# Block transposes on VectorE for Q, gate and up, and W_down's products directly behind the last PV

## The chip, the cores and the metric

The kernel runs on one core of a Trainium2 chip. The metric is device time in microseconds (us) of one execution. Five engines matter here: PE (TensorE: matrix products, with PEld for its weight loads), DVE (VectorE), ACT (ScalarE), POOL (GpSimd) and SP (SyncE, which only issues the transfers here). Sixteen DMA engines move data from HBM to SBUF. Engines run their own instruction streams in order and meet only at semaphores. A line such as L344 is line 344 of the kernel's file.

## The reference

One decode step of a transformer block with attention and a gated FFN in parallel; 4 sequences, one new token each. bf16 in and out.

```python
xn = layernorm(x)                                  # x: [4, 1, 512]
q  = xn @ wq                                       # 512 x 4096: 32 heads of 128
k, v = the last 4096 of 16384 cached rows, 8 kv heads (4 query heads share one)
o  = softmax(q k^T / sqrt(128)) v
g  = silu(xn @ w_gate)                             # 512 x 1792
u  = xn @ w_up                                     # 512 x 1792
out = x + o @ wo + (g * u) @ w_down                # wo: 4096 x 512, w_down: 1792 x 512
```

The cached rows that are read are 64 MiB; the five weight matrices are 13.25 MiB.

## The kernel before

**Transfers.** SP issues all large transfers on one queue, in this order: W_Q, K of steps 0 and 1, W_gate, W_up, then V and K in turn for the 16 steps (`ND`), W_down, the last V in two halves, and W_O in four pieces (`WO_CUTS` = 0, 16, 26, 30, 32: of the 32 row blocks of W_O the pieces hold 16, 10, 4 and 2). A step takes one kv head of two sequences, 2 MiB of K and 2 MiB of V. K and V have two buffers each. SP waits for `s_tr` (the transposes of K two steps back) before it issues a K, and for `s_pv` (the products with V of the step before) before it issues a V. The last V and W_O stand behind the wait for `s_pv` = 16.

**Start.** Layernorm on four partitions, four small transposes to `XnT`, then Q: 32 products of 512 columns (L360 from L374; L360 is the line of the helper `mm`, so most products have it), in four column groups of the PE array, so that partition 32j+b of a PSUM bank holds sequence b's heads of group j. Since the later products need Q with the head's 128 elements on the partitions, the two banks are copied to `QB` as bf16 (ACT L266 and DVE L287 side by side), turned by eight transposes on PE (L378), and spread into `QZ` by four small copies on DVE (L294).

**Steps.** The loop on PE transposes K (L390), copied to `KT` by DVE (L302), takes scores (L360, tile `ps_s`), shifts them by the maxima, ACT takes the exponential (L269), and PE multiplies by V (tile `ps_o`). `norm` on DVE (L318 to L322) divides by the denominators and writes one head group into `OT`.

**End.** Behind the loop, PE runs the rest of the last steps in this written order:

1. products with V, first-half sums and shift of steps still open;
2. gate (16 products of 512 columns) and up (16 more), again in four column groups: partition 32j+b holds sequence b's features of group j. Of a row of W_gate the columns are taken as `(m u)`: four neighbours (`u`), then a step of 14 elements (`m`); group 3 repeats two of the 14 feature blocks so that all groups have 512 columns;
3. x into the accumulator `ps_acc`, the last step's denominators and 64 products with V;
4. wait `s_gu`; four transposes of `gu` (L468); wait `s_nrm`; four transposes of `OT` (L472); wait `s_ob`; four small products that spread `OB` (L360, tile `ps_kt<-oB,rep`);
5. wait `s_guT`; 28 products with W_down; wait `s_op`; 64 products with W_O, each piece behind its own semaphore `d_wo`. Both write `ps_acc`, two column groups at a time.

ACT takes exp(-gate) from PSUM (L271, 128 x 512). DVE makes silu(gate)*up from it in four operations on 128 x 512: add one (L337), reciprocal (L339), multiply by gate (L341), multiply by up with the write in another order (L344). Only partitions 32j to 32j+3 of each 32 hold data. Then, in this order, the last `norm`, the copy `OB` (L349), the copy `guT` (L351), the copy `OP` (L353), and the copy of the result to `y` (L355), which SP and ACT write out.

Of the kernel before, what the change touches and what calls it, by code (L numbers as in the profile page):

```python
# [3 lines left out]
BF16 = mybir.dt.bfloat16  # L4
FP32 = mybir.dt.float32
ALU = mybir.AluOpType
ACT = mybir.ActivationFunctionType
# [3 lines left out]
def bass_parallel_sum__sliding_block_cached__swiglu_ffn__decode_kernel(  # L11
# [12 lines left out]
    B, _, D = A_x.shape  # L24
    _, HKV, Sk, Dh = A_k_cache.shape
    HQ = A_wq.shape[1] // Dh
# [3 lines left out]
    NC = D // 128  # L30
    NF = F // 128
    REP = HQ // HKV
# [3 lines left out]
    C = 2 * REP  # L36
# [23 lines left out]
    KT = sb("kT", [128, 2 * HKN], BF16)  # L60
    P = sb("p", [128, 2 * PS], BF16)
    QZ = sb("qz", [128, ND, WIDE], BF16)
    ident = sb("ident", [128, 128], BF16)
# [15 lines left out]
    st_std = sb("st_std", [B, 1], FP32)  # L79
    st_rstd = sb("st_rstd", [B, 1], FP32)  # L80
    XnT = sb("xnT", [128, NC, 32], BF16)
    QB = sb("qB", [128, 2, 512], BF16)
    den = sb("den", [128, C], FP32)
    OT = sb("oT", [128, B, REP + HQ], BF16)
    OB = sb("oB", [32, B, Dh], BF16)
    OP = sb("oP", [128, NO, B], BF16)
    ex = WQ[:, 0:1024].bitcast(FP32)
    gu = sb("gu", [128, 4, 128], BF16)
    guT = sb("guT", [128, 4, 128], BF16)
    I4 = sb("i4", [B, B], FP32)  # L90
    I4w = sb("i4w", [B, 64], BF16)
    y = sb("y_sb", [128, 256], BF16)
# [9 lines left out]
    O_wide = ps_O[:, 0:WIDE]  # L102
    den_ps = ps_O[:, 128:256]
    xT_ps = ps_acc[:, 0:NC * B]
    q_ps = kt_ps[2]
    mt_ps = ps_acc[0:C, 0:128]
    gate_ps = ps_kt[0][:]
    up_ps = ps_kt[1][:]
    gu_ps = kt_ps[2][:, B:2 * B, :]
    tr_ps = kt_ps[2][0:32, 0:B, :]  # L110
    op_ps = ps_kt[3][:, 0:B * 32]

    def sem(name):
        return nc.alloc_semaphore(name=name)
    d_x = sem("d_x")
    d_wq = sem("d_wq")
    d_wg = sem("d_wg")
    d_wu = sem("d_wu")
    d_wd = sem("d_wd")
# [13 lines left out]
    s_xT = sem("s_xT")  # L133
    s_xnT = sem("s_xnT")
    s_q = sem("s_q")
    s_qb = sem("s_qb")
    s_qt = sem("s_qt")
    s_gu = sem("s_gu")
    s_gt = sem("s_gt")
    s_qz = sem("s_qz")  # L140
    s_tr = sem("s_tr")
# [9 lines left out]
    s_gate = sem("s_gate")  # L151
    s_ex = sem("s_ex")
    s_up = sem("s_up")
    s_guT = sem("s_guT")
# [20 lines left out]
    with nc.Block() as block:  # L175
# [78 lines left out]
        @block.scalar  # L254
        def _(eng):
            eng.dma_start(X[:], x_ap).then_inc(d_x, 16)
            eng.wait_ge(s_xc, 1)
            eng.activation(xc[:], X[:], ACT.Identity, bias=st_neg[:, 0:1], scale=float(D))
            eng.drain()
            eng.activation(xsq[:], xc[:], ACT.Square, accum_out=st_sum[:, 0:1]).then_inc(s_ss, 1)  # L260
            eng.wait_ge(s_var, 1)
            eng.activation(st_std[:], st_var[:], ACT.Sqrt).then_inc(s_std, 1)
            eng.wait_ge(s_rs, 1)
            eng.activation(xn[:], xc[:], ACT.Identity, scale=st_rstd[:, 0:1]).then_inc(s_xn, 1)  # L264
            eng.wait_ge(s_q, 1)
            eng.activation(QB[:, 0, :], ps_kt[0][:], ACT.Identity).then_inc(s_qb, 1)  # L266
            for d in range(-1, ND):
                eng.wait_ge(s_sh, d + 2)
                eng.activation(P[:, d % 2 * PS:d % 2 * PS + SN], ps_S[d % 2][:], ACT.Exp, scale=SCALE).then_inc(s_p, 1)  # L269
            eng.wait_ge(s_gate, 1)  # L270
            eng.activation(ex, gate_ps, ACT.Exp, scale=-1.0).then_inc(s_ex, 1)  # L271
            eng.wait_ge(s_y, 1)
            eng.dma_start(out_ap[1], y[64:64 + B, :]).then_inc(d_out, 16)

        @block.vector
        def _(eng):
# [6 lines left out]
            eng.wait_ge(s_xT, 1)  # L283
            eng.wait_ge(s_const, 1)
            eng.tensor_copy(XnT[:, :, 0:B], xT_ps.rearrange("p (c b) -> p c b", b=B)).then_inc(s_xnT, 1)
            eng.wait_ge(s_q, 1)
            eng.tensor_copy(QB[:, 1, :], ps_kt[1][:]).then_inc(s_qb, 1)  # L287
            eng.wait_ge(s_qt, 1)

            qv = q_ps.rearrange("p (n h) (j x) -> p j n x h", n=2, x=32)  # L290
            qz = QZ[:].rearrange("p (j n i) c -> p j n i c", n=2, i=2)
            for n in range(2):
                for i in range(2):
                    last = eng.tensor_copy(qz[:, :, n, i, 0:C].rearrange("p j (m h) -> p j m h", m=2),  # L294
                                           qv[:, :, n, 2 * i:2 * i + 2, :])
            last.then_inc(s_qz, 1)
            eng.engine_nop().then_inc(s_ev, NG)

# [17 lines left out]
            def norm(n, b, r):  # L316
                eng.wait_ge(s_pv, n)
                eng.tensor_reduce(den[:], den_ps.rearrange("p (t c) -> p c t", c=C), AX.X, ALU.add)  # L318
                eng.drain()
                eng.reciprocal(den[:], den[:])  # L320
                eng.drain()
                eng.tensor_tensor(OT[:, 2 * b:2 * b + 2, ds(r * REP, REP)],  # L322
                                  O_ps.rearrange("p (j h) -> p j h", j=2),
                                  den[:].rearrange("p (j h) -> p j h", j=2), ALU.mult).then_inc(s_nrm, 1)

            with eng.Fori(0, ND // 2) as r:
                for b in range(2):
# [5 lines left out]
            row_max(1, ND + 1)  # L333
            shift(ND + 1)
            norm(ND + 1, 0, ND // 2)
            eng.wait_ge(s_ex, 1)
            eng.tensor_scalar(ex, ex, 1.0, None, ALU.add)  # L337
            eng.drain()
            eng.reciprocal(ex, ex)  # L339
            eng.drain()  # L340
            eng.tensor_tensor(ex, gate_ps, ex, ALU.mult)  # L341
            eng.wait_ge(s_up, 1)
            eng.drain()
            eng.tensor_tensor(gu[:].rearrange("p u m -> p m u"), up_ps.rearrange("p (m u) -> p m u", u=4),  # L344
                              ex.rearrange("p (m u) -> p m u", u=4), ALU.mult).then_inc(s_gu, 1)
            norm(ND + 2, 1, ND // 2)

            eng.wait_ge(s_t4, 1)
            eng.tensor_copy(OB[:], tr_ps).then_inc(s_ob, 1)  # L349
            eng.wait_ge(s_gt, 1)  # L350
            eng.tensor_copy(guT[:], gu_ps).then_inc(s_guT, 1)  # L351
            eng.wait_ge(s_pm, 1)
            eng.tensor_copy(OP[:].rearrange("p c b -> p b c"), op_ps.rearrange("p (b c) -> p b c", b=B)).then_inc(s_op, 1)  # L353
            eng.wait_ge(s_acc, 1)
# [3 lines left out]
        def _(eng):  # L358
            def mm(o, l, r, start=False, stop=True):
                return eng.matmul(o, l, r, start=start, stop=stop, skip_group_check=True)  # L360
# [3 lines left out]
            for c in range(NC):  # L364
                last = eng.transpose(xT_ps[:, c * B:(c + 1) * B],  # L365
                                     xn[:].rearrange("b (p c) -> b c p", c=NC)[:, c, :], I4[:])
            last.then_inc(s_xT, 1)
            eng.wait_ge(s_xnT, 1)
            eng.wait_ge(d_wq, 16)
            for c in range(NC):  # L370
                for n in range(2):
                    for j in range(4):
                        a = (c * HQ + 8 * j + 4 * n) * Dh
                        last = mm(ps_kt[n][32 * j:32 * j + 32, :], XnT[:, c, :], WQ[:, a:a + 512], start=(c == 0))  # L374
            last.then_inc(s_q, 1)
            eng.wait_ge(s_qb, 2)
            for k in range(8):
                last = eng.transpose(q_ps[:, k, :], QB[:, k // 4, 128 * (k % 4):128 * (k % 4 + 1)], ident[:])  # L378
            last.then_inc(s_qt, 1)

            def mask(bank):
                return mm(ps_S[bank][:].rearrange("p (t c) -> p t c", c=C), mkr[:],
# [65 lines left out]
            pv(0, 1, ND + 1)  # L448
            shift(1, ND + 1)


            T0 = (0, 4, 8, NF - 4)
            for w, o, done, d in ((WG, ps_kt[0], s_gate, d_wg), (WU, ps_kt[1], s_up, d_wu)):
                eng.wait_ge(d, 16)
                for c in range(NC):
                    wv = w[:, c, :].rearrange("p (m t) -> p m t", t=NF)
                    for j in range(4):
                        last = mm(o[32 * j:32 * j + 32, :].rearrange("p (m u) -> p m u", u=4), XnT[:, c, :],
                                  wv[:, :, T0[j]:T0[j] + 4], start=(c == 0))
                last.then_inc(done, 1)  # L460
            for n in range(2):
                mm(ps_acc[64 * n:64 * n + 64, 0:256], I4w[:], X[:, 256 * n:256 * n + 256], start=True)
            pv(1, 0, (8 * ND + 16, ND + 1))
            eng.wait_ge(d_vz, 16)
            pv(1, 1, None)
            eng.wait_ge(s_gu, 1)
            for u in range(4):
                last = eng.transpose(gu_ps[:, u, :], gu[:, u, :], ident[:])  # L468
            last.then_inc(s_gt, 1)
            eng.wait_ge(s_nrm, ND + 2)  # L470
            for i in range(B):
                last = eng.transpose(  # L472
                    tr_ps[:, i, :],
                    OT[:, i, REP:], ident[:])
            last.then_inc(s_t4, 1)
            eng.wait_ge(s_ob, 1)
            for e in range(REP):
                last = mm(op_ps.rearrange("p (b c) -> p b c", b=B), rep[:, e, :], OB[:, :, 32 * e:32 * e + 32],
                          start=(e == 0))
            last.then_inc(s_pm, 1)  # L480
            eng.wait_ge(s_guT, 1)
            eng.wait_ge(d_wd, 16)
            for t in range(NF):
                j = min(t // 4, 3)
                u = t - T0[j]
                for n in range(2):
                    mm(ps_acc[64 * n:64 * n + B, 0:256], guT[:, u, 32 * j:32 * j + B],
                       WD[:, t, 256 * n:256 * n + 256])
            eng.wait_ge(s_op, 1)
            for c in range(NO):  # L490
                if c in WO_CUTS:
# [32 lines left out]
```

## Time and profile before

| | |
|---|---|
| median of 3 runs | 202.76 us (201.81 to 202.96) |
| the profiled execution's own time | 203.49 us |
| its span, first to last instruction | 201.8 us |
| PE, DVE, ACT, POOL busy | 83%, 59%, 9%, 5% of the span |
| HBM read | 81.01 MB, 402 GB/s over the span |
| mean granted TensorE clock | 0.958 |

In the page of the profile, the span is cut in 40 slices of 5.04 us. A digit is the busy share of a slice in tenths; PEclk is the clock granted to PE in tenths of full speed. A row of the chain of waits reads: start, duration, what ran (or what was waited for). A row of the timeline adds the number of instructions and, in brackets, how long the engine had been idle and what ended that. The views of the trace are from the profiled execution alone.

### The profile page before, as it was taken

The numbers are of one execution on the slowest core, as the hardware profiler recorded it, in microseconds if no ns is written. First come the engines' busy times: TensorE is split into PE (matmuls) and PEld (weight loads), VectorE is DVE, ScalarE is ACT, GpSimd is POOL, SyncE is SP. The second block draws the span as 40 slices with busy tenths as digits, with TensorE's granted clock in tenths as the row PEclk, the third lists the DMA queues.
The fourth block names the chain that finished last, engine by engine and source line by source line (L and its number), as shares of the span: only waits on it lengthen the run. The fifth ranks groups of instructions, "written<-read, shape, count | busy, mean of one in ns | idle before, by whom it ended". The sixth has DMA issues, their size and how long they took to land.

```text
span 201.8 us, 7765 instructions
## 1 busy us (share of the span) xinstructions
PE 167.1 (83%) x3470; PEld 143.2 (71%) x3470; DVE 119.3 (59%) x250; ACT 17.6 (9%) x27; POOL 10.3 (5%) x23
## 2 busy tenths in 40 slices
PE   0137998859999989889898989898989898986395
PEld 0113896758988978788788878887878787854263
DVE  1003757644777575757666767676767676738700
ACT  6303010101010101010100101010101010110000
POOL 8920000000000000000000000000000000000000
PEclk9999699988999999999999999999999999999559
DMA  7999999999999999999999999999999999999800
GB/s 248 448 393 429 436 424 426 437 422 429 406 426 439 435 422 439 432 422 435 432 432 426 439 435 422 439 432 422 435 432 432 426 439 435 413 435 421 373 12 1
DMA packets 5934, 81.10 MB, mean 402 GB/s; under 512 B 668, under 2 KB 680, under 8 KB 936
## 3 DMA queue, kind: packets, MB, share of 16 engines
q1 hardware_dynamic: 5912, 81.01, 94.4%
q8 instruction: 5, 0.08, 0.2%
q10 hardware_dynamic: 16, 0.01, 0.0%
q14 instruction: 1, 0.01, 0.0%
HBM read 81.01 MB, written 0.00 MB: 402 GB/s over the span
## 4 chain that ended last, share of the span: by engine, by line
DMA 51%; PE 40%; DVE 6%; issue 2%; ACT 0%; DVEq 0%
DMA kbuf<-in_A_k_cache_dram 44%; PE ps_kt L390 17%; PE ps_s L360 9%; DMA wq_sb<-in_A_wq_dram 6%; PE ps_o L360 6%; PE ps_acc L360 5%; PE ps_kt L360 3%; DVE wq_sb L339 2%; DVE kT L302 1%; DVE gu L344 1%; DVE rm L307 0%; DVE qB L287 0%; DVE wq_sb L341 0%; PE ps_kt L378 0%; ACT wq_sb L271 0%
## 5 line engine op out<-in xcount | busy, mean ns | idle before, releaser
L302 DVE COPY kT<-ps_kt 128x1024 bf16<-128x1024 bf16 x128 | 79.8, 683 | 27.3 <-PE ps_kt L390 27.2
L390 PE MATMUL ps_kt<-ident,kbuf 128*128 128x128 bf16 x1024 | 64.4, 222 | 10.6 <-DMA kbuf<-in_A_k_cache_dram 10.5
L390 PEld LDWEIGHTS ps_kt<-ident,kbuf 128*128 128x128 bf16 x1024 | 58.8, 99 | 15.6 <-issue 15.6
L360 PE MATMUL ps_o<-p,vbuf 128*128 128x64 bf16 x1120 | 39.4, 195 | 0.0
L360 PEld LDWEIGHTS ps_o<-p,vbuf 128*128 128x128 bf16 x1120 | 36.2, 99 | 1.2
L360 PEld LDWEIGHTS ps_s<-qz,kT 128*128 128x128 bf16 x1024 | 31.4, 98 | 7.6 <-issue 4.6
L360 PE MATMUL ps_s<-qz,kT 128*128 x1024 | 34.8, 192 | 2.0 <-issue 0.8
L269 ACT ACTIVATE p<-ps_s 128x512 bf16<-128x512 f32 x17 | 10.2, 597 | 152.0 <-PE ps_s L360 152.0
L307 DVE TENSOR_REDUCE rm<-ps_s 128x8 bf16<-128x512 f32 x17 | 11.8, 691 | 19.3 <-PE ps_s L360 19.3
L360 PE MATMUL ps_kt<-wq_sb,xnT 128*32 128x512 bf16 x32 | 3.4, 609 | 5.4 <-DMA wq_sb<-in_A_wq_dram 5.4
L360 PE MATMUL ps_o<-p,ones 128*128 128x128 bf16 (+1 forms) x69 | 6.9, 220 | 0.8 <-DVE qz L294 0.7
L360 PE MATMUL ps_s<-mkc,mkr 2*128 2x512 bf16 x17 | 6.7, 393 | 0.0
L365 PE MATMUL ps_acc<-i,xn 4*128 4x4 f32 x4 | 0.6, 255 | 7.2 <-ACT xn L264 7.2
L360 PE MATMUL ps_s<-dg,ones 8*128 8x512 bf16 x17 | 6.5, 385 | 0.0
L360 PEld LDWEIGHTS ps_kt<-wq_sb,xnT 128*32 128x32 bf16 x32 | 1.3, 140 | 6.9 <-issue 6.9
L318 DVE TENSOR_REDUCE den<-ps_o 128x8 f32<-128x128 f32 x18 | 5.1, 281 | 1.6 <-PE ps_o L360 1.6
L287 DVE CAST qB<-ps_kt 128x512 bf16<-128x512 f32 x1 | 0.7, 691 | 8.7 <-PE ps_kt L360 8.7
L365 PEld LDWEIGHTS ps_acc<-i,xn 4*128 4x128 f32 x4 | 0.6, 210 | 7.2 <-issue 7.2
L360 PEld LDWEIGHTS ps_o<-p,ones 128*128 128x128 bf16 x69 | 4.5, 98 | 1.3 <-issue 0.8
L211 POOL MEMSET vbuf<- 128x6144 f32 x1 | 5.2, 5222 | 0.0
L360 PE MATMUL ps_acc<-wo_sb,oP 128*4 128x256 bf16 x64 | 5.1, 334 | 0.0
L355 DVE CAST y_sb<-ps_acc 128x256 bf16<-128x256 f32 x1 | 0.4, 426 | 7.5 <-PE ps_acc L360 7.5
(69 smaller groups left out, 62.7 us busy)
## 6 DMA issues: line engine op xcount, KB each, us to landing
kbuf<-in_A_k_cache_dram SPq DMA_DIRECT2D x16, 2048.0 KB, 12.6
vbuf<-in_A_v_cache_dram SPq DMA_DIRECT2D x15, 2048.0 KB, 11.2
wq_sb<-in_A_wq_dram SPq DMA_DIRECT2D x1, 4096.0 KB, 12.3
vbuf<-in_A_v_cache_dram SPq DMA_DIRECT2D x2, 1024.0 KB, 9.2
wo_sb<-in_A_wo_dram SPq DMA_DIRECT2D x1, 2048.0 KB, 14.5
wg_sb<-in_B_w_gate_dram SPq DMA_DIRECT2D x1, 1792.0 KB, 25.8
wu_sb<-in_B_w_up_dram SPq DMA_DIRECT2D x1, 1792.0 KB, 29.4
wd_sb<-in_B_w_down_dram SPq DMA_DIRECT2D x1, 1792.0 KB, 15.0
```

Source lines behind the costliest of these rows:

```text
L211: eng.memset(VB[:, HKN:].bitcast(FP32), 0.0)
L269: eng.activation(P[:, d % 2 * PS:d % 2 * PS + SN], ps_S[d % 2][:], ACT.Exp, scale=SCALE).then_inc(s_p, 1)
L287: eng.tensor_copy(QB[:, 1, :], ps_kt[1][:]).then_inc(s_qb, 1)
L302: eng.tensor_copy(KT[:, u * HKN + 1024 * g:u * HKN + 1024 * (g + 1)], kt_ps[g].rearrange("p a b -> p (a b)")).then_inc(s_ev, 1)
L307: eng.tensor_reduce(RM[:], ps_S[bank][:].rearrange("p (t c) -> p c t", c=C), AX.X, ALU.max).then_inc(s_rm, 1)
L318: eng.tensor_reduce(den[:], den_ps.rearrange("p (t c) -> p c t", c=C), AX.X, ALU.add)
L339: eng.reciprocal(ex, ex)
L344: eng.tensor_tensor(gu[:].rearrange("p u m -> p m u"), up_ps.rearrange("p (m u) -> p m u", u=4), ex.rearrange("p (m u) -> p m u", u=4), AL ...
L355: eng.tensor_copy(y[:], ps_acc[:, 0:256]).then_inc(s_y, 1)
L360: return eng.matmul(o, l, r, start=start, stop=stop, skip_group_check=True)
L365: last = eng.transpose(xT_ps[:, c * B:(c + 1) * B], xn[:].rearrange("b (p c) -> b c p", c=NC)[:, c, :], I4[:])
L390: last = eng.transpose(kt_ps[g][:, k, :], KB[:, a:a + 128], ident[:])
```

## The change

Q, gate and up are turned by VectorE's 32x32 block transposes, straight out of PSUM as float32. A block transpose turns each block of 32 partitions by 32 columns in place: element (32j+b, 32t+m) goes to (32j+m, 32t+b).

- **Q.** The products are ordered so that the first bank is complete after 16 of the 32 (with `s_q` raised for each bank), and take their columns in blocks of 32 neighbours, so that after the block transposes (two, 128 x 512) each head's 128 elements lie on the 128 partitions. Two copies spread the result into `QZ`. The copies to `QB` on ACT and DVE, the eight PE transposes and two of the four copies into `QZ` go.
- **Gate and up.** 16 products each of 448 columns instead of 512 (nothing repeated). Columns are taken as `(t m)`: the inner index `m` runs over 32 columns with a step of 14 elements (28 bytes), each column by itself. DVE turns gate to `gT` and, once up is there, up to `uT` (128 x 448 each, into the storage of W_Q). The four batch columns of each of 14 feature blocks are then 56 columns on all 128 partitions. ACT's exponential now reads `gT` and waits for its transpose (`s_gt`) instead of the gate products; add, reciprocal and both multiplications are on 56 columns, and the last writes `guT` directly. The four PE transposes of `gu` and the copy to `guT` go.
- **Order at the end.** W_down's 28 products stand right behind the last products with V, ahead of the transposes of `OT`; before, they stood ahead of W_O's.

```diff
-    QB = sb("qB", [128, 2, 512], BF16)
...
-    ex = WQ[:, 0:1024].bitcast(FP32)
-    gu = sb("gu", [128, 4, 128], BF16)
-    guT = sb("guT", [128, 4, 128], BF16)
+    ex = sb("ex", [128, NF, B], FP32)
+    guT = sb("guT", [128, NF, B], BF16)
+    qT = KT[:, 0:2048].bitcast(FP32)
+    gT = WQ[:, 0:NF * 64].bitcast(FP32)
+    uT = WQ[:, NF * 64:NF * 128].bitcast(FP32)
...
-    gate_ps = ps_kt[0][:]
-    up_ps = ps_kt[1][:]
+    gate_ps = ps_kt[0][:, 0:NF * 32]
+    up_ps = ps_kt[1][:, 0:NF * 32]
...
 # ACT
-            eng.wait_ge(s_q, 1)
-            eng.activation(QB[:, 0, :], ps_kt[0][:], ACT.Identity).then_inc(s_qb, 1)
             for d in range(-1, ND):
...
-            eng.wait_ge(s_gate, 1)
-            eng.activation(ex, gate_ps, ACT.Exp, scale=-1.0).then_inc(s_ex, 1)
+            eng.wait_ge(s_gt, 1)
+            eng.activation(ex[:], gT.rearrange("p (t b) -> p t b", b=32)[:, :, 0:B], ACT.Exp, scale=-1.0).then_inc(s_ex, 1)
...
 # DVE, start
-            eng.wait_ge(s_q, 1)
-            eng.tensor_copy(QB[:, 1, :], ps_kt[1][:]).then_inc(s_qb, 1)
-            eng.wait_ge(s_qt, 1)
...
             for n in range(2):
-                for i in range(2):
-                    last = eng.tensor_copy(qz[:, :, n, i, 0:C].rearrange("p j (m h) -> p j m h", m=2),
-                                           qv[:, :, n, 2 * i:2 * i + 2, :])
+                eng.wait_ge(s_q, n + 1)
+                eng.transpose(qT[:, 512 * n:512 * n + 512], ps_kt[n][:])
+            eng.drain()
+            for i in range(2):
+                last = eng.tensor_copy(
+                    QZ[:].rearrange("p (k i) c -> p k i c", i=2)[:, :, i, 0:C].rearrange("p k (m h) -> p k m h", m=2),
+                    qT.rearrange("p (k h x) -> p k x h", h=REP, x=32)[:, :, 2 * i:2 * i + 2, :])
             last.then_inc(s_qz, 1)
...
 # DVE, end
             norm(ND + 1, 0, ND // 2)
+
+            eng.wait_ge(s_gate, 1)
+            eng.transpose(gT, gate_ps).then_inc(s_gt, 1)
+            eng.wait_ge(s_up, 1)
+            eng.transpose(uT, up_ps)
             eng.wait_ge(s_ex, 1)
-            eng.tensor_scalar(ex, ex, 1.0, None, ALU.add)
-            eng.drain()
-            eng.reciprocal(ex, ex)
-            eng.drain()
-            eng.tensor_tensor(ex, gate_ps, ex, ALU.mult)
-            eng.wait_ge(s_up, 1)
-            eng.drain()
-            eng.tensor_tensor(gu[:].rearrange("p u m -> p m u"), up_ps.rearrange("p (m u) -> p m u", u=4),
-                              ex.rearrange("p (m u) -> p m u", u=4), ALU.mult).then_inc(s_gu, 1)
+            eng.tensor_scalar(ex[:], ex[:], 1.0, None, ALU.add)
+            eng.drain()
+            eng.reciprocal(ex[:], ex[:])
+            eng.drain()
+            eng.tensor_tensor(ex[:], gT.rearrange("p (t b) -> p t b", b=32)[:, :, 0:B], ex[:], ALU.mult)
+            eng.drain()
+            eng.tensor_tensor(guT[:], uT.rearrange("p (t b) -> p t b", b=32)[:, :, 0:B], ex[:],
+                              ALU.mult).then_inc(s_guT, 1)
             norm(ND + 2, 1, ND // 2)
...
-            eng.wait_ge(s_gt, 1)
-            eng.tensor_copy(guT[:], gu_ps).then_inc(s_guT, 1)
...
 # PE, start
-            for c in range(NC):
-                for n in range(2):
+            for n in range(2):
+                for c in range(NC):
+                    wv = WQ[:, c * HQ * Dh:(c + 1) * HQ * Dh].rearrange("p (n h d) -> p n h d", n=2, d=Dh)
                     for j in range(4):
-                        a = (c * HQ + 8 * j + 4 * n) * Dh
-                        last = mm(ps_kt[n][32 * j:32 * j + 32, :], XnT[:, c, :], WQ[:, a:a + 512], start=(c == 0))
-            last.then_inc(s_q, 1)
-            eng.wait_ge(s_qb, 2)
-            for k in range(8):
-                last = eng.transpose(q_ps[:, k, :], QB[:, k // 4, 128 * (k % 4):128 * (k % 4 + 1)], ident[:])
-            last.then_inc(s_qt, 1)
+                        last = mm(ps_kt[n][32 * j:32 * j + 32, :].rearrange("p (h d) -> p h d", d=32), XnT[:, c, :],
+                                  wv[:, n, :, 32 * j:32 * j + 32], start=(c == 0))
+                last.then_inc(s_q, 1)
...
 # PE, end
-            T0 = (0, 4, 8, NF - 4)
-            for w, o, done, d in ((WG, ps_kt[0], s_gate, d_wg), (WU, ps_kt[1], s_up, d_wu)):
+            for w, o, done, d in ((WG, gate_ps, s_gate, d_wg), (WU, up_ps, s_up, d_wu)):
                 eng.wait_ge(d, 16)
                 for c in range(NC):
-                    wv = w[:, c, :].rearrange("p (m t) -> p m t", t=NF)
+                    wv = w[:, c, :].rearrange("p (m t) -> p t m", t=NF)
                     for j in range(4):
-                        last = mm(o[32 * j:32 * j + 32, :].rearrange("p (m u) -> p m u", u=4), XnT[:, c, :],
-                                  wv[:, :, T0[j]:T0[j] + 4], start=(c == 0))
+                        last = mm(o[32 * j:32 * j + 32, :].rearrange("p (t m) -> p t m", t=NF), XnT[:, c, :],
+                                  wv[:, :, 32 * j:32 * j + 32], start=(c == 0))
                 last.then_inc(done, 1)
...
             pv(1, 1, None)
-            eng.wait_ge(s_gu, 1)
-            for u in range(4):
-                last = eng.transpose(gu_ps[:, u, :], gu[:, u, :], ident[:])
-            last.then_inc(s_gt, 1)
+            eng.wait_ge(s_guT, 1)
+            eng.wait_ge(d_wd, 16)
+            for t in range(NF):
+                for n in range(2):
+                    mm(ps_acc[64 * n:64 * n + B, 0:256], guT[:, t, :], WD[:, t, 256 * n:256 * n + 256])
             eng.wait_ge(s_nrm, ND + 2)
...
             last.then_inc(s_pm, 1)
-            eng.wait_ge(s_guT, 1)
-            eng.wait_ge(d_wd, 16)
-            for t in range(NF):
-                j = min(t // 4, 3)
-                u = t - T0[j]
-                for n in range(2):
-                    mm(ps_acc[64 * n:64 * n + B, 0:256], guT[:, u, 32 * j:32 * j + B],
-                       WD[:, t, 256 * n:256 * n + 256])
             eng.wait_ge(s_op, 1)
```

More of the change, by code (lines that the diff above doesn't have):

```diff
@@ L104, in bass_parallel_sum__sliding_block_cached__swiglu_ffn__decode_kernel @@
     xT_ps = ps_acc[:, 0:NC * B]
-    q_ps = kt_ps[2]
     mt_ps = ps_acc[0:C, 0:128]
-    gate_ps = ps_kt[0][:]
-    up_ps = ps_kt[1][:]
-    gu_ps = kt_ps[2][:, B:2 * B, :]
+    gate_ps = ps_kt[0][:, 0:NF * 32]
+    up_ps = ps_kt[1][:, 0:NF * 32]
     tr_ps = kt_ps[2][0:32, 0:B, :]
@@ L135, in bass_parallel_sum__sliding_block_cached__swiglu_ffn__decode_kernel @@
     s_q = sem("s_q")
-    s_qb = sem("s_qb")
-    s_qt = sem("s_qt")
-    s_gu = sem("s_gu")
     s_gt = sem("s_gt")
@@ L285, in _ @@
             eng.tensor_copy(XnT[:, :, 0:B], xT_ps.rearrange("p (c b) -> p c b", b=B)).then_inc(s_xnT, 1)
-            eng.wait_ge(s_q, 1)
-            eng.tensor_copy(QB[:, 1, :], ps_kt[1][:]).then_inc(s_qb, 1)
-            eng.wait_ge(s_qt, 1)
-            qv = q_ps.rearrange("p (n h) (j x) -> p j n x h", n=2, x=32)
-            qz = QZ[:].rearrange("p (j n i) c -> p j n i c", n=2, i=2)
-            for n in range(2):
-                for i in range(2):
-                    last = eng.tensor_copy(qz[:, :, n, i, 0:C].rearrange("p j (m h) -> p j m h", m=2),
-                                           qv[:, :, n, 2 * i:2 * i + 2, :])
+            for n in range(2):
+                eng.wait_ge(s_q, n + 1)
[5 more added lines that the diff above has]
+                    qT.rearrange("p (k h x) -> p k x h", h=REP, x=32)[:, :, 2 * i:2 * i + 2, :])
             last.then_inc(s_qz, 1)
```

## The prediction

> **What bounds the kernel now.** I read the DMA share first (the page's slices, then stretches of two microseconds), then the chain of waits from its end, then the timeline of the last 20 us. The slices of the DMA queue are full from the start, and the last transfer ends before the kernel does:
>
> ```profile
> DMA  7999999999999999999999999999999999999800
> 190.00:192.00 2.00, 1.49 (x14) 0.84 (x14) 1.18 (x3) 0.00 (x0) 0.00 (x0) 0.50 0.64 251
> 192.00:194.00 2.00, 2.00 (x24) 1.22 (x20) 0.00 (x1) 0.00 (x0) 0.00 (x0) 0.50 0.06 13
> wu_sb<-in_B_w_up_dram SPq DMA_DIRECT2D x1, 1792.0 KB, 29.4
> wo_sb<-in_A_wo_dram SPq DMA_DIRECT2D x1, 2048.0 KB, 14.5
> wo_sb<-in_A_wo_dram SPq DMA_DIRECT2D x1, 1280.0 KB, 16.9
> wo_sb<-in_A_wo_dram SPq DMA_DIRECT2D x1, 512.0 KB, 17.7
> wo_sb<-in_A_wo_dram SPq DMA_DIRECT2D x1, 256.0 KB, 17.8
> 173.20 0.59 SPq L233 DMA_DIRECT2D wo_sb<-in_A_wo_dram  x1
> 173.83 1.39 SPq L233 DMA_DIRECT2D wo_sb<-in_A_wo_dram  x3
> ```
>
> In the windows' rows the last two columns are DMA share and GB/s; a landing is counted from the issue. W_O is issued at 173.20, 173.83, about 174.3 and 174.8 (1.39 us over three), so its pieces land at 187.7, 190.7, 192.0 and 192.6. Up to there transfers set the pace. What follows is a tail: the last product with W_O ends at 199.5, 6.9 us behind the data. The chain of waits (start, us, what) says why:
>
> ```profile
> 180.15 1.28 PE ps_kt L360 x13
> 181.45 0.61 ACT wq_sb L271
> 182.08 0.43 DVE wq_sb L337
> 182.58 3.35 DVE wq_sb L339
> 186.01 0.69 DVE wq_sb L341
> 186.78 2.44 DVE gu L344
> 189.27 0.61 PE ps_kt L468 x4
> 189.87 0.55 PE ps_kt L472 x4
> 190.45 0.42 DVE oB L349
> 190.92 0.60 PE ps_kt L360 x4
> 191.52 7.97 PE ps_acc L360 x92
> 199.52 0.43 DVE y_sb L355
> ```
>
> From the gate's last product at 181.43 to 189.22 the end waits for ACT and DVE on 512 columns; the short steps and the products with W_down and W_O come behind that. PE meanwhile finished and stood still, and its clock fell (the column ahead of the DMA share is the granted clock):
>
> ```profile
> 182.97 2.03 PE L360 MATMUL ps_o<-p,vbuf 128*128 128x64 bf16 x64
> 181.22 1.35 PE L360 MATMUL ps_kt<-wu_sb,xnT 128*32 128x512 bf16 x16
> 180.08 1.33 PE L360 MATMUL ps_kt<-wg_sb,xnT 128*32 128x512 bf16 x16
> 191.45 3.15 PE L360 MATMUL ps_acc<-wd_sb,guT 128*4 128x256 bf16 x28
> 194.39 5.08 PE L360 MATMUL ps_acc<-wo_sb,oP 128*4 128x256 bf16 x64
> 183.80:187.20 3.40, 1.20 (x41) 1.07 (x37) 3.25 (x3) 0.00 (x0) 0.00 (x0) 0.98 0.98 417
> 187.20:190.60 3.40, 1.15 (x8) 0.69 (x8) 2.53 (x5) 0.00 (x0) 0.00 (x0) 0.50 0.98 408
> 194.00:197.40 3.40, 3.40 (x36) 2.13 (x34) 0.00 (x0) 0.00 (x0) 0.00 (x0) 0.51 0.00 0
> 98.40:101.80 3.40, 2.55 (x67) 2.34 (x63) 1.55 (x3) 0.00 (x0) 0.00 (x0) 1.00 1.00 429
> ```
>
> W_down's 28 products start within 2.94 us (191.45 to 194.39), 105 ns each at clock 0.50. At full clock I take half, 52.5 ns: with 29 of W_O's at 105 ns up to 197.4 and 35 at 52.5 ns, the last would start at 199.2 and end 0.3 later, which is where the chain has it (199.49).
>
> **The start of the kernel: no effect, either way.** On the path from Q's products to `QZ`, one 0.69 us copy stays as a block transpose, eight PE transposes (0.6 us) go, and four copies become two. Q may be ready about 1 us earlier, or later if the block transposes are dear. The cover:
>
> ```profile
> 3.25 0.44 SPq L239 DMA_DIRECT2D wu_sb<-in_B_w_up_dram  x1
> 24.01 0.55 SPq L225 DMA_DIRECT2D vbuf<-in_A_v_cache_dram  x1
> ```
>
> W_up, issued at 3.25, lands at 32.65. The first V is issued at 24.01, behind PE's first steps, so the queue holds work for 8.6 us more when SP gets there. An earlier SP only queues earlier; a later one costs nothing up to 8.6 us, and what follows it in the queue would then be late. The last landing stays at 192.6. ACT loses a copy nobody else waited for. No transfer is added, removed or moved past another.
>
> **Gate and up.** 32 products remain, of 448 columns. By the columns 2.5 us (180.08 to 182.57) becomes 2.2, and the gate ends at 181.3. But each column now lies 28 bytes from the next, where four neighbours were read before each such step. No product of this trace steps at every column. If all the time went to the steps (128 per product before, 448 now), they would cost 3.5 times as much, 8.0 us instead of 2.3 (start to start), 5.7 us more. I take the old times, 181.43 and 182.57, since the nearest row is this very read pattern with a step at every fourth column.
>
> [...]
>
> **FFN on DVE.** The rows for the sizes:
>
> ```profile
> L341 DVE TENSOR_TENSOR wq_sb<-ps_kt,wq_sb 128x512 f32<-128x512 f32 x1 | 0.7, 692 | 0.1
> L355 DVE CAST y_sb<-ps_acc 128x256 bf16<-128x256 f32 x1 | 0.4, 426 | 7.5 <-PE ps_acc L360 7.5
> L287 DVE CAST qB<-ps_kt 128x512 bf16<-128x512 f32 x1 | 0.7, 691 | 8.7 <-PE ps_kt L360 8.7
> L320 DVE RECIPROCAL den<-den 128x8 f32<-128x8 f32 x18 | 3.7, 203 | 1.3
> L322 DVE TENSOR_TENSOR oT<-ps_o,den 128x8 bf16<-128x8 f32 x2 | 0.3, 166 | 0.1
> L318 DVE TENSOR_REDUCE den<-ps_o 128x8 f32<-128x128 f32 x18 | 5.1, 281 | 1.6 <-PE ps_o L360 1.6
> ```
>
> Two float32 copies out of PSUM give 1.04 ns a column plus 0.16 us. A block transpose of 448 columns at that price takes 0.63 us. No transpose on DVE is in the trace; the dearest rows per column are the rewritten product (2.43 us for 512: 4.8 ns) and the reciprocal (3.35 us: 6.5 ns), which would make it 2.1 or 2.9 us. The cheapest is the addition (0.43 us for 512), which would make it 0.38. I take 0.63, as the data come from the same place in the same type.
>
> So `gT` at 182.1; ACT's exponential on 56 columns (0.6 us for 512) beside the wait for up; `uT` from 182.6 to 183.25. Add 0.2 (0.43 for 512), reciprocal 0.5 (203 ns for 8 columns, 6.3 ns a column more), two multiplications 0.22 each (between 166 and 692 ns), four gaps of 0.07: 1.4 us. `guT` is ready at 184.65. PE's products with V end at 185.0. The FFN, 7.8 us on the path, is hidden behind them with 0.35 us to spare; the cover gone, each microsecond of it is on PE's path.
>
> **PE's end.** W_down from 185.0, 28 x 52.5 ns: 186.5. DVE runs `norm` meanwhile (0.28 + 0.20 + 0.17 and gaps, about 0.9: 185.95), so nothing waits behind `s_nrm`. Transposes of `OT` 0.4 (0.55 at the low clock), `OB` 0.45, spreading 0.4, `OP` 0.45 to 0.5: W_O can begin at 188.25. Alone it would take 64 x 52.5 ns and end at 191.85. But its pieces end that: 32 products until 189.95, then wait for 190.7, 20 until 191.75, wait for 192.0, 8 until 192.4, wait for 192.6, four more: the last starts at 192.8 and ends 0.27 later, 193.05. The slack of PE's own path to that is 1.2 us. What is late next is thus W_O's data.
>
> The end moves from 199.5 to 193.05, by 6.45 us; the copy to `y` and the output follow as before. The profiled execution took 203.49 (span 201.8 and 1.7 around it): 197.04. It is 0.73 above the median of the runs, 202.76; off that, 196.3.
>
> **Rivals.**
>
> *The clock falls all the same (chance 0.22).* PE now has short idle times from 186.9 to 190.7. The trace's stretches of 3.4 us show the clock kept with 2.55 us busy and lost after 1.20; the stretch 187.2 to 190.6 would have about 2.1. Falling at 190.6, 32 products at 105 ns lie behind the 190.7 landing: end at 194.4, saving 5.1 us, 197.6. Falling already at 187.2: 195.4, 198.7. [...]
>
> *The 28-byte step costs much (0.17).* At the upper end, 5.7 us more, the products with V end at 190.7, `guT` is there, and by the sums above W_O ends at 197.5: saving 2.0, 200.8. At half of it, 197.9. The four-neighbour pattern's mild pace (2.5 us for 32) speaks against the top end.
>
> *The block transpose is dear, and it gets slower (0.04).* Both stand in DVE's queue ahead of all FFN work and the last `norm`. With T for each, `guT` comes at 183.4 + 2(T - 0.63). PE is then idle behind the V products, the clock falls as it did before, and W_down takes 2.94 us again. With T = 2.9 (the reciprocal's price) `guT` is at 188, and W_O ends within 0.7 us of 199.5. Beyond about T = 3.2 us (7 ns a column) the kernel is slower; at 4, about 203.5. No DVE row reaches that price per column.
>
> *Nothing is gained (0.02):* something else, such as `norm`, holds PE until 189; no row points to it.
>
> **How the numbers follow.** The forecast (W_O's last landing sets the end) has 0.55: 196.3, its own range 195.2 to 197.0, from the spread of the runs before (202.96 to 201.81, about 1 us below the median). The range reaches through the clock rival and the lower half of the step rival: 195.2 to 199.6. A difference of 0.5%, 1 us, is about what a measurement here can tell from none. Faster: 0.55 + 0.22 + 0.17, less 0.01 for a dear step and a low clock together: 0.93. Same 0.03, slower 0.04.
>
> **What would show it.** Right: no stretch of idle PE between V's and W_down's products; `guT` before 185.5; W_O's products in four groups, each behind a landing, at clock 1.00. Wrong: gate and up over 3.5 us; clock 0.50 while W_O runs (each falsifies its own term); a last landing far from 192.6, which would undo the sum; transposes on DVE over 1.5 us.

## The result, and the profile after

The changed kernel takes 200.16 us (median of 5 runs, 200.09 to 200.24) against 202.76 (201.81 to 203.04): ratio 0.988, 95% interval 0.985 to 0.991. It is faster, as forecast (1.2%, and the two sets of runs do not overlap), but by 2.6 us and not by 6.5, and lies 0.6 us above the range. The profiled execution took 200.16 us with a span of 198.4.

The chain of waits from the gate on (start, us, what):

```profile
180.23 6.57 PE ps_kt L354 x26
186.81 0.23 PE ps_acc L354 x2
187.03 2.20 PE ps_o L354 x68
189.23 1.62 PE ps_acc L354 x28
190.85 0.23 PE ps_kt L463 x4
191.11 0.42 DVE oB L345
191.58 0.41 PE ps_kt L354 x4
192.01 0.45 DVE oP L347
192.50 3.68 PE ps_acc L354 x64
196.20 0.42 DVE y_sb L349
```

No DVE work on the FFN is left in it, and W_down's products (189.23) follow V's without a gap. The 6.6 us at its head are the products of gate and up, where 1.3 us of the gate alone stood before. In the timeline of the changed kernel, and then in its windows of 2 us (granted clock, DMA share and GB/s in the last three columns):

```profile
180.16 3.42 PE L354 MATMUL ps_kt<-wg_sb,xnT 128*32 128x448 bf16 x16
183.38 3.43 PE L354 MATMUL ps_kt<-wu_sb,xnT 128*32 128x448 bf16 x16
183.62 0.65 DVE L330 STREAM_TRANSPOSE wq_sb<-ps_kt 128x448 f32<-128x448 f32 x1 [2.87 <-PE ps_kt L354]
186.85 0.65 DVE L332 STREAM_TRANSPOSE wq_sb<-ps_kt 128x448 f32<-128x448 f32 x1 [2.57 <-PE ps_kt L354]
187.65 0.50 DVE L336 RECIPROCAL ex<-ex 128x56 f32<-128x56 f32 x1
188.52 0.22 DVE L340 TENSOR_TENSOR guT<-wq_sb,ex 128x56 bf16<-128x56 f32 x1
```

```profile
190.00:192.00 2.00, 1.46 (x24) 0.97 (x20) 0.48 (x2) 0.00 (x0) 0.00 (x0) 1.00 0.70 273
192.00:194.00 2.00, 1.50 (x28) 1.23 (x30) 0.44 (x1) 0.00 (x0) 0.00 (x0) 1.00 0.02 6
```

Sixteen products take 3.22 us from start to start (180.16 to 183.38), 0.805 us for each four that run in the four column groups; before, it was 1.14 us (180.08 to 181.22), 0.285 for four. The 32 together need 4.2 us more. The block transposes cost 0.65 us each, the reciprocal 0.50 instead of 3.35, and `guT` is there at 188.74, half a microsecond ahead of W_down. The clock stays at 1.00 to the end (in every window of 2 us from 180 to 196), and the last transfers land as before (DMA share 0.02 from 192 on).

### The profile page after: what moved, and what is told of

It reads as the page before. It is cut to its first block, busy times and chain, and to the rows that moved or that the text cites. A ratio compares the mean times of both kernels' runs of the same rounds, so it can differ in the third digit from the quotient of the medians.

```text
span 198.4 us, 7741 instructions
## 1 busy us (share of the span) xinstructions
PE 167.4 (84%) x3458; PEld 141.5 (71%) x3458; DVE 115.6 (58%) x250; ACT 16.6 (8%) x26; POOL 10.3 (5%) x23
## 4 chain that ended last, share of the span: by engine, by line
DMA 51%; PE 42%; DVE 3%; issue 2%; DVEq 0%
DMA kbuf<-in_A_k_cache_dram 45%; PE ps_kt L382 17%; PE ps_s L354 9%; PE ps_o L354 7%; DMA wq_sb<-in_A_wq_dram 6%; PE ps_kt L354 5%; PE ps_acc L354 4%; DVE kT L294 1%; DVE kT L282 0%; DVE rm L299 0%; DVE oP L347 0%; DVE y_sb L349 0%; DVE oB L345 0%; DVE qz L285 0%; PE ps_kt L463 0%
## 5 line engine op out<-in xcount | busy, mean ns | idle before, releaser
L382 PE MATMUL ps_kt<-ident,kbuf 128*128 128x128 bf16 x1024 | 65.6, 224 | 10.6 <-DMA kbuf<-in_A_k_cache_dram 10.5
L382 PEld LDWEIGHTS ps_kt<-ident,kbuf 128*128 128x128 bf16 x1024 | 59.9, 100 | 15.9 <-issue 15.9
L354 PE MATMUL ps_o<-p,vbuf 128*128 128x64 bf16 x1120 | 38.7, 194 | 0.0
L354 PEld LDWEIGHTS ps_o<-p,vbuf 128*128 128x128 bf16 x1120 | 35.5, 98 | 1.2
L282 DVE STREAM_TRANSPOSE kT<-ps_kt 128x512 f32<-128x512 f32 x2 | 1.4, 716 | 8.1 <-PE ps_kt L354 8.1
L304 DVE TENSOR_REDUCE m<-ps_acc 8x1 f32<-8x128 f32 x17 | 4.6, 268 | 0.3 <-PE ps_acc L354 0.3
L314 DVE TENSOR_TENSOR oT<-ps_o,den 128x8 f32 (+1 forms) x18 | 3.0, 167 | 2.9 <-issue 2.7
## 6 DMA issues: line engine op xcount, KB each, us to landing
wo_sb<-in_A_wo_dram SPq DMA_DIRECT2D x1, 2048.0 KB, 14.5
```

The source lines that it names most:

```text
L282: eng.transpose(qT[:, 512 * n:512 * n + 512], ps_kt[n][:])
L304: eng.tensor_reduce(m8[:], mt_ps, AX.X, ALU.max)
L382: last = eng.transpose(kt_ps[g][:, k, :], KB[:, a:a + 128], ident[:])
```

## The experiments

All times are medians; the kernel before ran beside each group: 203.0 us in the first (201.96 to 203.6), 202.8 in the second, 202.6 in the third. "Four products" means one in each column group, timed from start to start.

**How far apart the columns lie.** Three kernels compute the same and differ from the changed one in which features of gate and up form a block, with W_down's rows dealt out to match. First, blocks of 128 neighbours, 32 for each column group:

```diff
-    wd_ap = B_w_down.rearrange("(p t) n -> p t n", t=NF)
+    wd_ap = B_w_down.rearrange("(t p) n -> p t n", t=NF)
...
-                    wv = w[:, c, :].rearrange("p (m t) -> p t m", t=NF)
+                    wv = w[:, c, :].rearrange("p (t m) -> p t m", t=NF)
```

> The edit: gate and up take their columns in runs of 32 neighbours (64 bytes), and W_down is loaded with its rows dealt out to match; all else as in the changed kernel. Theory LINES: the moving operand's read costs a fixed time for every 16-byte line that a stream visits, about 1.8 ns: 448 columns at 28 bytes are 448 lines, 0.806 us per four products measured; the kernel before visits 160 lines in 512 columns, 0.285 us measured; both give 1.8. Runs of 64 bytes are 56 lines and no limit, so the columns set the pace: about 0.19 us per four, 1.5 us for all 32 products instead of 6.5. The products with V then end near 184.3, W_O can start at 187.8, and W_O's last landing (192.7) ends the kernel: last product at 193.1, span 195.3, time 197.0. W_down in 1 KB pieces instead of 14 KB may cost the queue up to 1 us: 198.0. Rival TAIL: the products' pace is not what is missing, and something behind them (block transposes, the short steps) holds the end: not under 199.5.

Measured: 197.68 us (197.51 to 198.25), ratio to before 0.9745 (0.972 to 0.977). Four products take 0.19 us. The TAIL rival falls.

Then columns 4 and 14 bytes apart (`s` = 2 and 7):

```diff
-    wd_ap = B_w_down.rearrange("(p t) n -> p t n", t=NF)
+    wd_ap = B_w_down.rearrange("(a p s) n -> p a s n", p=128, s=2)
...
-                    wv = w[:, c, :].rearrange("p (m t) -> p t m", t=NF)
+                    wv = w[:, c, :].rearrange("p (a m s) -> p a s m", m=128, s=2)
...
```

> The edit: as the run with runs of 32 neighbours, but the columns of gate and up lie 4 bytes apart (every second element), W_down in 2 KB pieces. LINES: four columns share a 16-byte line, 112 lines at 1.8 ns are 0.20 us per four products, the same as with neighbours: all 32 in 1.6 us, time 197.0 to 197.6. Rival STEP: any column that is not the neighbour of the last costs as much as in the changed kernel, whatever the distance: 0.81 us per four, 6.5 us in all, time 200.2.

> The edit: the same with columns 14 bytes apart (every seventh element). LINES: 32 columns cover 436 bytes, so 28 lines, 392 for 448 columns, 0.71 us per four products instead of 0.81: 5.6 us in all, 0.8 us less than in the changed kernel: time 199.4. STEP: 0.81 us per four, time 200.2. [...]

Measured: 197.49 us (197.31 to 198.17; ratio 0.974, 0.970 to 0.978) and 199.29 us (199.2 to 199.55). The gate's and up's products in the timelines with neighbours, with 4 and with 14 bytes, one fence for each kernel:

```profile
180.00 0.94 PE L354 MATMUL ps_kt<-wg_sb,xnT 128*32 128x448 bf16 x16
180.77 0.93 PE L354 MATMUL ps_kt<-wu_sb,xnT 128*32 128x448 bf16 x16
```

```profile
180.47 0.94 PE L354 MATMUL ps_kt<-wg_sb,xnT 128*32 128x448 bf16 x16
181.25 0.93 PE L354 MATMUL ps_kt<-wu_sb,xnT 128*32 128x448 bf16 x16
```

```profile
180.22 2.96 PE L354 MATMUL ps_kt<-wg_sb,xnT 128*32 128x448 bf16 x16
182.99 2.99 PE L354 MATMUL ps_kt<-wu_sb,xnT 128*32 128x448 bf16 x16
```

A quarter of the distance between the two starts is the time of four products. The lines are those of the LINES theory: aligned stretches of 16 bytes, counted once for each in which a product's run of columns has a column.

| columns read as | 16-byte lines per product | four products, us | ns per line |
|---|---|---|---|
| 32 neighbours | 56 | 0.19 | (columns: 0.43 ns each) |
| 4 bytes apart | 112 | 0.195 | (columns: 0.44 ns each) |
| four neighbours, then 28 bytes (before, 512 columns) | 160 | 0.285 | 1.78 |
| 14 bytes apart | 392 | 0.69 | 1.77 |
| 28 bytes apart (changed kernel) | 448 | 0.805 | 1.80 |

STEP falls: columns 4 bytes apart take 0.195 us per four products, neighbours 0.19. That a line has 16 bytes was assumed by the theory, and the five rows agree with it: with lines of 8 bytes the steps of 14 and 28 would cost the same, with 32 the former half; it costs 0.86 (0.69 against 0.805 us; 392 lines to 448 are 0.875). A line that holds more than one column costs as well: in the old pattern every visited line holds two or four columns of the stream (every fourth group of neighbours straddles two lines), and its 512 columns take 0.285 us instead of the 0.22 us that 0.43 ns each would make. A line costs as much as 4.2 neighbouring columns (1.8 by 0.43 ns). With four columns in each line (4 bytes apart) lines and columns cost about the same, so this row tells nothing of the price of a line; the old pattern, with 3.2 columns per line on average, was already slower than its columns.

**Whether the 1 KB pieces of W_down cost.** The first of these with W_down loaded as ever:

```diff
-    wd_ap = B_w_down.rearrange("(t p) n -> p t n", t=NF)
+    wd_ap = B_w_down.rearrange("(p t) n -> p t n", t=NF)
```

> The edit: as the run with runs of 32 neighbours, but W_down is loaded as in the changed kernel, in 14 KB pieces; the features of gate and up then meet other rows of W_down than theirs, and the output is not the reference's. Theory PIECES: the 1 KB pieces of W_down cost the queue 0.5 to 1 us, which is why W_O's last landing came at 193.8 there and at 192.7 in the changed kernel; here it comes at 192.7 again, the last product ends at 193.1 to 193.2, time 197.0. Rival: the landings scatter by themselves, and the time is that of the runs with small pieces, 197.5 to 197.7.

Measured: 197.55 us (197.03 to 198.19). The profiled execution, the fastest, has the forecast's last stretch:

```profile
184.24 1.70 PE L354 MATMUL ps_acc<-wd_sb,guT 128*4 128x256 bf16 x28
185.76 0.39 PE L463 MATMUL ps_kt<-ident,oT 128*32 128x128 bf16 x4
187.86 1.91 PE L354 MATMUL ps_acc<-wo_sb,oP 128*4 128x256 bf16 x32 [0.81 <-DMA wo_sb<-in_A_wo_dram]
190.82 2.21 PE L354 MATMUL ps_acc<-wo_sb,oP 128*4 128x256 bf16 x32 [1.05 <-DMA wo_sb<-in_A_wo_dram]
```

W_O's products wait for their data (in brackets), the last ends at 193.03, the span is 195.3. But the median is that of the runs with small pieces, within 0.2 us, and all three scatter by about 1 us: the rival holds, and PIECES is not shown. A run further below says the same: in the kernel before with PE kept busy, which loads W_down in 14 KB pieces, W_O's last piece lands 18.8 us behind its issue, against 17.7 here and 18.9 in the first run with 1 KB pieces. What makes W_O's landings scatter stays open.

**Whether a stream pays by itself or four together.** In the changed kernel, the order of the products turned round (`for j` outside `for c`), and the same with neighbours:

```diff
-                for c in range(NC):
-                    for j in range(4):
+                for j in range(4):
+                    for c in range(NC):
```

> The edit: in the changed kernel, gate's and up's products run through the four row blocks of one column group before the next group, so that neighbouring products cannot run beside each other in different column groups. Theory ALONE: each stream pays the 1.8 ns per line by itself, so a product takes 0.8 us also alone: 16 x 0.8 = 12.9 us per matrix, 25.8 for both instead of 6.5, time near 219. Rival SHARED: the four streams share one path of about 0.45 ns per line, so that a stream alone takes 0.2 us per product: 16 x 0.2 = 3.2 us per matrix as before, time 200.2.

> The edit: runs of 32 neighbours (and W_down loaded to match), with the products of one column group one behind another. SHARED, as the serial run with the 28-byte step had it: a stream alone goes at one column in about 0.45 ns with either pattern, since the 28-byte step costs nothing alone and the four streams only lose their side-by-side: 16 x 0.2 = 3.2 us per matrix, time 199.8 to 200.2. Rival: products of one column group overlap as well, and the serial run with the 28-byte step showed nothing: then 0.2 us per four as with neighbours in four groups, 0.8 us per matrix, time 197.6.

Measured: 200.07 and 197.64 us in a single run each, the times without the turned order, and the same 0.81 and 0.19 us per four (28-byte step first, then neighbours):

```profile
180.03 3.44 PE L354 MATMUL ps_kt<-wg_sb,xnT 128*32 128x448 bf16 x16
183.25 3.48 PE L354 MATMUL ps_kt<-wu_sb,xnT 128*32 128x448 bf16 x16
```

```profile
180.23 0.97 PE L354 MATMUL ps_kt<-wg_sb,xnT 128*32 128x448 bf16 x16
180.99 0.96 PE L354 MATMUL ps_kt<-wu_sb,xnT 128*32 128x448 bf16 x16
```

The first looked like SHARED; the second shows that it told nothing, since products that the program puts one behind another in one column group go four at a time as well (in the trace of the first, the weight loads come in fours, each four within 0.16 us and 0.8 us behind the four before: at 180.82 and 181.62, at 184.07 and 184.87). How they do so is not shown. Both kernels rest on a wrong premise. So the stream was measured alone, with weights 128 columns wide, in the kernel before:

```diff
+            for u in range(8):
+                mm(ps_kt[3][:, 0:448], ident[:], WQ[:, 8192 + 448 * u:8192 + 448 * u + 448], start=True)
+            wv = WG[:, 0, :].rearrange("p (m t) -> p t m", t=NF)
+            for u in range(8):
+                mm(ps_kt[3][:, 0:448].rearrange("p (t m) -> p t m", t=NF), ident[:],
+                   wv[:, :, 32 * (u % 4):32 * (u % 4) + 32], start=True)
             eng.wait_ge(s_gu, 1)
```

> The edit: in the kernel before, in the place of the 66 filling products: eight products on the full array (128 weight columns, so no column groups) of 448 neighbouring columns, then eight of 448 columns 28 bytes apart, all into an unused bank. A product on the full array has one stream of columns. Theory ALONE: that stream pays 1.8 ns per line, 0.19 us for a product of neighbours and 0.81 us for a stepping one. Rival SHARED: the 28-byte step only costs where four column groups read at once; 0.19 us and 0.20 us. The filling shortens or delays the end by what it takes: with SHARED 3.1 us of filling, time near 200.5; with ALONE 8 us, PE busy until 193, time near 203.

```profile
184.78 1.68 PE L360 MATMUL ps_kt<-wq_sb,ident 128*128 128x448 bf16 x8
186.30 6.59 PE L360 MATMUL ps_kt<-wg_sb,ident 128*128 128x448 bf16 x8
190.00:192.00 2.00, 2.00 (x4) 0.33 (x3) 0.00 (x0) 0.00 (x0) 0.00 (x0) 1.00 0.54 214
192.00:194.00 2.00, 1.85 (x10) 0.70 (x8) 0.11 (x1) 0.00 (x0) 0.00 (x0) 0.55 0.02 8
```

Eight products of neighbours take 1.52 us start to start (0.19 each), eight stepping ones 6.41 us up to the next transpose at 192.71: 0.80 each. ALONE holds, 1.79 ns a line. The whole took 206.07 us in its single run, 3 us above the expected, since the clock fell at 192 (last rows; further below) and W_down's products took 3.15 us again.

**What the clock alone is worth.** The kernel before, with its 512-column FFN, and PE kept busy while it waits:

```diff
+            for u in range(66):
+                mm(ps_kt[3][:, 0:128], ident[:], ones[:], start=True)
             eng.wait_ge(s_gu, 1)
```

> The edit: the kernel before, with 66 products of 128 columns into an unused PSUM bank put behind the last products with V, ahead of the wait for gate*up; nothing else changes, and DVE's 7.8 us on 512 columns stay. Theory CLOCK: a large part of what the change won is that PE does not stand still and keeps its full clock: W_down 1.5 us instead of 2.9, W_O 3.4 instead of 4.9, short steps 0.6 less. By the chain, W_down then starts at 191.1 and W_O ends at 196.2 instead of 199.5: time 200.2, as the changed kernel, and the spread of the kernel before (2 us) goes to under 0.5 us. Rival FFN: the work on 512 columns is what costs, the clock little: 202.5 to 203.5, with the spread.

Measured: 200.23 us (200.02 to 200.34), ratio 0.987 (0.984 to 0.991). The chain of waits of this kernel:

```profile
182.48 3.35 DVE wq_sb L339
185.91 0.69 DVE wq_sb L341
186.68 2.44 DVE gu L344
...
190.62 0.39 PE ps_kt L360 x4
191.01 5.14 PE ps_acc L360 x92
196.17 0.42 DVE y_sb L355
```

Two of its windows:

```profile
189.00:191.00 2.00, 1.18 (x14) 0.72 (x16) 1.23 (x6) 0.00 (x0) 0.00 (x0) 1.00 0.96 385
193.00:195.00 2.00, 2.00 (x42) 1.61 (x38) 0.00 (x0) 0.00 (x0) 0.00 (x0) 1.00 0.05 9
```

All of DVE's work is still in it, the clock is 1.00 where the kernel before had 0.50, and W_down's and W_O's 92 products take 5.14 us instead of 7.97. Products whose result nobody uses gain as much as the whole change. And the spread of 1.9 us (201.77 to 203.69 in 15 runs of the kernel before) shrinks to 0.3.

The converse, the costly reading put into the kernel before:

```diff
-            eng.tensor_tensor(gu[:].rearrange("p u m -> p m u"), up_ps.rearrange("p (m u) -> p m u", u=4),
-                              ex.rearrange("p (m u) -> p m u", u=4), ALU.mult).then_inc(s_gu, 1)
+            eng.tensor_tensor(gu[:].rearrange("p u m -> p (u m)"), up_ps, ex, ALU.mult).then_inc(s_gu, 1)
...
-                    wv = w[:, c, :].rearrange("p (m t) -> p m t", t=NF)
+                    wv = w[:, c, :].rearrange("p (m t) -> p t m", t=NF)
...
-                                  wv[:, :, T0[j]:T0[j] + 4], start=(c == 0))
...
+                                  wv[:, T0[j]:T0[j] + 4, :], start=(c == 0))
```

> The edit: the kernel before, with gate and up read as in the changed kernel, each column 28 bytes from the next (512 columns); the multiplication by up then writes in order. Its products take 0.92 us per four, 7.4 us instead of 2.3, and PE is busy until 190.1. CLOCK: gate*up is ready at 190.0 (0.69 us for the last multiplication, since it writes in order), PE is never idle for long, and with the full clock W_O ends near 197.5: time 201.5 although the products take 5 us longer. Rival FFN: gate's end is 2.5 us later, the last multiplication 1.7 us shorter, so all behind it comes 0.8 us later: 204.0.

Measured: 201.39 us (201.12 to 201.59), ratio 0.993 (0.9905 to 0.995): faster, though the products take 7.4 us:

```profile
180.14 3.88 PE L359 MATMUL ps_kt<-wg_sb,xnT 128*32 128x512 bf16 x16
183.84 3.85 PE L359 MATMUL ps_kt<-wu_sb,xnT 128*32 128x512 bf16 x16
```

Four products take 0.925 us, 512 lines at 1.81 ns. PE has no long idle time left (0.51 us at most from 180 to its last product), and the clock stayed at 1.00 in the whole profile. Two things differ here, the reading and the multiplication's writing; the 1.7 us that the second saves are in both forecasts, and only CLOCK's comes out. FFN falls as a rival in both runs.

**The order of W_down.** In the changed kernel, its 28 products back ahead of W_O's:

```diff
             pv(1, 1, None)
-            eng.wait_ge(s_guT, 1)
-            eng.wait_ge(d_wd, 16)
-            for t in range(NF):
...
             last.then_inc(s_pm, 1)
+            eng.wait_ge(s_guT, 1)
+            eng.wait_ge(d_wd, 16)
+            for t in range(NF):
...
             eng.wait_ge(s_op, 1)
```

> The edit: in the changed kernel, W_down's 28 products go back to their old place, behind the products that spread OB and ahead of W_O's. In the changed kernel the last norm (0.85 us behind the products with V) is covered by W_down's 1.5 us, and in the old place W_down's would be covered against the copies OB and OP. By the chain: transposes of OT at 190.1 instead of 190.7, spreading done at 191.4, W_down 191.4 to 192.9, W_O from 192.9 instead of 192.5: 0.4 us later, time 200.6. Rival: the order is worth the whole 1.5 us (201.7), or nothing (200.2).

Measured: 200.61 us (200.31 to 200.71), 0.45 above the changed kernel. Its chain again carries `norm` in the open ([0.90] is PE's wait for it):

```profile
190.16 0.40 PE L458 MATMUL ps_kt<-ident,oT 128*32 128x128 bf16 x4 [0.90 <-DVE oT L314]
191.39 1.69 PE L354 MATMUL ps_acc<-wd_sb,guT 128*4 128x256 bf16 x28
192.92 3.66 PE L354 MATMUL ps_acc<-wo_sb,oP 128*4 128x256 bf16 x64
```

**Q.** The changed kernel with Q's two copies and eight PE transposes of before:

```diff
-                eng.transpose(qT[:, 512 * n:512 * n + 512], ps_kt[n][:])
+            eng.tensor_copy(QB[:, 1, :], ps_kt[1][:]).then_inc(s_qb, 1)
...
+                last = eng.transpose(q_ps[:, k, :], QB[:, k // 4, 128 * (k % 4):128 * (k % 4 + 1)], ident[:])
```

> The edit: the changed kernel with Q as in the kernel before (two copies, eight transposes on PE, four copies; products in the old order). The prediction's step: no effect, since W_up's landing at 32.6 leaves the queue work for 8.6 us when SP issues the first V: time 200.2 within 0.2. Rival: the earlier start of the steps is worth its 0.5 us: 200.7.

Measured: 200.18 us (199.96 to 200.23). No effect.

## Why the prediction was wrong, step by step

- **What bounds the kernel: right.** The transfers end where they did; W_O's pieces land 14.5 to 17.8 us behind their issues (173.3 to 174.9), the last at 192.7 (192.6 forecast).
- **The start has no effect: right.** SP issued the first V at 23.90 instead of 24.01; the run with the old Q took the same time.
- **Gate and up: wrong, and this is the step that failed.** "I take the old times", 2.3 us for the 32 products, because the nearest row had a step at every fourth column. Measured 6.44 us. The upper end, 8.0, counted the steps alone; the count that fits is that of lines, 160 against 448, at about 1.8 ns each, and 0.285 us times 448/160 is 0.80. The prediction's own sign of being wrong, gate and up over 3.5 us, came. The old pattern was not a mild one with a step in it, but already slower than its columns, and a row that is itself slowed by the thing in question can't stand for its lower end.
- **FFN on DVE: right.** Block transposes 0.65 us (0.63), exponential 0.25, add 0.15, reciprocal 0.50 (0.5), multiplications 0.22 each; 1.24 us behind `uT` (1.4). It stayed hidden behind V's products.
- **PE's end: right, 4.2 us later.** From V's last product to W_O's last it was to take 6.85 us without waiting for data; it took 6.95 (189.23 to 196.18). V's end came at 189.2 for 185.0, which uses up the slack of 1.2 us and moves the end from 193.05 to 196.18: of the 6.45 us, 3.3 remain between the profiles. Where the reading is cheap, W_O's landings do set the end, with a span of 195.3 in the fastest profile against 195.35 by the sum.
- **The 0.73 us taken off: wrong.** The sum gave 197.04, and the runs with cheap reading took 197.5 to 197.7 at the median, 197.03 at best. The profile lay above its median as one of the runs with the lowest mean clock: at its 0.958 the kernel before took 203.5 to 203.7 us in four other runs, at 0.966 203.1 to 203.5, and 201.8 to 203.3 in the rest. That the low clock in the tail made this spread is likely, though no trace of a second run shows it. With the clock kept up, the spread is gone (the filler run), and so is the reason to take anything off; the changed kernel's profile and median agree to the hundredth.
- **How the miss adds up.** From the forecast of 196.3 to the measured 200.16 it is 3.86 us: 3.0 from gate and up (4.2 less the slack of 1.2), 0.73 from what was taken off, 0.13 from PE's end. By the prediction's own sums, the 28-byte step at its measured price alone gives 199.3, still inside the range; with the 0.73 us left in, 200.04, outside.
- **Rivals.** The clock did not fall; that rival fell. The 28-byte step, at 0.17, is what came, at about three quarters of its upper end (4.2 of 5.7 us), where the range meant to cover its lower half. The dear block transpose fell.
- **What had not been seen:** the low clock alone cost the kernel before as much as the whole change gained. The prediction had its price in the sum (105 against 52.5 ns), but put the gain down to the FFN's 7.8 us. In the changed kernel PE's own products took the FFN's place on the path: W_down could start at 189.23, and `gu` had been ready at 189.22. Up to there nothing was gained; all 3.3 us between the two profiles come behind it, where 6.95 us replace 10.3 at the full clock with fewer short steps. The filler run gets from 189.11 to its last product at 196.15 in the same 7.0 us, with the old steps and order: the gain can be had by the clock alone.

The version with columns 4 bytes apart (197.49 us; with neighbours it is the same within the scatter) beats both kernels, by 5.5 us and by 2.7 us. It ends about 2.7 us of span behind W_O's last landing, most of it the copy and the write-out.

## What to carry to other kernels

Choose which features share a block so that the moving operand (the one that streams through PE) reads at least four bf16 columns from each 16 bytes (0.195 us per four products of 448 columns with four in each, against 0.805 with one), and deal out the next matrix's rows to match; no cost of that shows in these runs, and it was worth 2.5 to 2.7 us. Before a long elementwise chain is shortened, see what PE's clock does while it waits: filling the gap with throw-away products (200.23 us, clock 1.00 where it had been 0.50) was worth as much as the whole rewrite (200.16 us). A row that already suffers from an effect is no bound against that effect; count what it is made of (lines, not steps) and scale.

## What the runs showed of the hardware that was not expected

- In these kernels a matmul's stream pays about 1.8 ns for each 16-byte line that it visits (1.77 to 1.81 in the four patterns that are slower than their columns), by itself: a lone full-array product of 448 columns takes 0.19 us with neighbours and 0.80 us at 28 bytes; four column groups side by side are not slower (0.19 and 0.805 us).
- Products with 32 weight columns go four at a time even if the program puts them one behind another in one column group (0.19 us per four in either order).
- Busy, as the profile counts it, is not enough for the clock: in the one run with lone streams PE was busy without a gap from 186 to 192 (2.00 of 2.00) with stepping products, and the clock fell to 0.50 at 192.2, before the last of them was done. Four stepping streams kept it at 1.00 in the changed kernel (6.6 us) and in the kernel before with the costly reading (7.5 us). What the clock goes by is not shown.
- A write in another order costs DVE much: the multiplication by up took 2.43 us with its transposing write and 0.69 us for the same 512 columns in order (the run with the costly reading in the kernel before).
